# Spare products through the first routing of an attention and mixture-of-experts kernel, with two weight tiles loaded later and small steps in another order

## The chip, the cores and the metric

The kernel runs on one core of a Trainium2 chip. The metric is device time in microseconds (us): the time of one execution, as a median of several. The core's engines work side by side and wait for each other by semaphores: TensorE (PE in the profile, its weight loads PEld), VectorE (DVE), ScalarE (ACT), GpSimd (POOL) and SyncE (SP), which here issues most of the DMA transfers.

## The reference

Three stages follow one another, all in float32.

```python
def reference(**kwargs):
    ...
    attn_out = _attn_ref(**attn_kwargs)          # q, k, v: 4 x 8 heads x 768 x 64
    B, H, S, D = attn_out.shape
    x = np.ascontiguousarray(attn_out.transpose(0, 2, 1, 3)).reshape(B * S, H * D)
    x = _moe_ref(x=x, **moe_kwargs)              # 3072 tokens of 512, 8 experts, F = 1024
    return _moe2_ref(x=x, **moe2_kwargs)
```

`_attn_ref` is attention in chunks of 32 queries, each with a window of the keys around it and 8 memory keys. `_moe_ref` sends each token to one expert. The assignment is greedy over all 3072 x 8 logits, the largest first, and an expert is full with 384 tokens:

```python
    logits = x @ w_gate
    order = np.argsort(-logits.flatten())
    for idx in order:
        tok, e = (int(idx) // E, int(idx) % E)
        if assigned[tok] >= 0 or counts[e] >= cap:
            continue
        assigned[tok] = e
        counts[e] += 1
    ...
    for e in range(E):
        mask = assigned == e
        h = np.maximum(x[mask] @ w1[e], 0.0)
        out[mask] = h @ w2[e]
```

`_moe2_ref` sends each token to the two best of eight other experts, by noisy logits, and adds their weighted outputs.

## The kernel before, in words

Attention handles 24 tiles of 128 tokens, software-pipelined: for each tile a list of steps (scores, softmax, av, xtrans, logits, levac and so on) is issued in a fixed pattern, and its last tiles by the list `REST` (line 227), whose words are "step tile". `propose` and `tally` are steps that carry the first pieces of the first routing: VectorE's masks of the logits, and their counts on TensorE. Each tile of x leaves for DRAM in `xr`.

From there on `moe1` (line 1441) works with a planner, `Pipe` (line 73). It keeps a modelled time for each engine (`account`, `rdy`). The parts of the work are generators (`loads`, `lists1`, `gathers`, `splits`, `route` and others), and each yields the modelled time, or the condition, from which it wants to go on. `tick` lets those go on whose time has come by TensorE's modelled clock. The instructions of every engine are issued in the order in which the generators run, and each engine executes its own in that order. `until(cond, spare)` (line 197) is what the main loop does while TensorE has nothing to compute: with a `spare` tile it issues one spare product (a 128x128 tile of ones, `ones16`, times itself, into a PSUM tile that is overwritten later) and ticks; without one it only moves TensorE's modelled clock on by 50 ns and ticks. The main loop waits for the first expert's gathers without spares (line 1484), and for its tokens and weights with them.

The first routing is the `k == 0` pass of `route` (line 692). The experts are closed one after another, and a pass finds the next one to be full and the logit at which it is full, by a search over thresholds: VectorE compares all best logits `V` with a set of candidates (`GE`, in two halves for `k == 0`), TensorE counts them for each expert with 24 small products into `rps` (the masks are the stationary side, the one-hot `OH` the moving one), VectorE compares the counts with the capacity (`flf`), one product with `onesb` adds up over the partitions and spreads the sum, VectorE makes `d` and the next candidates `ci`. After the last round come `NQ` and its count, `est` (the expert's number, which SyncE reads with a TENSOR_LOAD and which sets the address of the first weights), `bE`, `at`, `T`, `bT`, and `shut`, which writes `L`, the logits with the closed expert masked off.

`lists1` (line 663) then makes the expert's token list: `l1pos` (two products), `lpos`, and in `slot_list` (line 613) the one-hots `sloh` and 24 products into `slps`; four small writes copy it into `idx`. `gather1` (line 1293) issues three indirect DMAs on GpSimd (`xg`), which fetch the tokens; for expert 0 GpSimd then writes `behind`, and SyncE reads it with a TENSOR_LOAD, so that later loads go out after the gathers. The gathered rows are transposed on TensorE (`tps`) and copied by ScalarE (`xT`).

`loads` (line 1017) brings each expert's weights in tiles `st0_0` to `st0_3` of 128 x 1024 (512 KB) for expert 0's first matrix, `st1` for its second. `split` turns them into a high and a low half in float16: ScalarE squares a tile and sums it (`junk`, `sq`), a product with `onesb` adds up (`tot`), VectorE makes a scale (`nt`, `i`, `s`, `i1c`), ScalarE copies the scaled tile to `w_0h` and so on, and VectorE or GpSimd writes the rest, `w_0l`. `mm1` multiplies `xT` with both halves into `m`; ScalarE and VectorE split the result into `hT`; `mm2_f32` (`m2f`) and `mm2` are the second products.

## Time and profile before

| | us |
|---|---|
| median of 3 runs | 1053.85 (1053.73 to 1054.35) |
| the profiled execution | 1061.16 |
| its span, first to last instruction | 1059.4 |
| TensorE busy in the span | 990.7 (94%) |
| VectorE busy | 643.4 (61%) |
| ScalarE busy | 460.4 (43%) |
| mean granted clock of TensorE | 0.969 of full speed |

Attention fills the first 130 us or so, the first routing goes on until expert 0's first product at 161 us, the first mixture of experts ends around 546 us and the second at the end of the span. In the timeline a row is a group of like instructions in succession, with its start, its time and their number; the bracket says how long the engine had been idle before it and what it then waited for. Rows of products after line 68 come from one helper that records every operation of the planner, so the tiles' names tell them apart. A granted clock of 1.00 is 2.4 GHz, one of 0.50 is 1.2 GHz.

### The profile page before, as it was taken

The page shows a single profiled execution, that of the slowest core. Times are in us where ns is not written, and L with a number is a line of the kernel's source. Part 1 is how long each engine was busy: PE and PEld are TensorE (multiplying, and loading weights), DVE is VectorE, ACT ScalarE, POOL GpSimd, SP SyncE. Part 2 cuts the span into 40 slices and gives each one's busy share as a digit, 9 for nine tenths or more (in the row PEclk, how much of TensorE's full clock was granted, in tenths as well). Part 3 has the DMA queues.
Part 4 walks back from the last instruction along what each step waited for, and adds up shares of the span by engine and source line. Part 5 has one row for each costly group of instructions (what it writes and reads, how often), then busy time and mean ns, then how long its engine had stood idle before and what let it go on. Part 6 is the DMA issues. An engine that isn't in the chain of part 4 may idle for free.

```text
span 1059.4 us, 21987 instructions
## 1 busy us (share of the span) xinstructions
PE 990.7 (94%) x8312; PEld 595.4 (56%) x8312; DVE 643.4 (61%) x2096; ACT 460.4 (43%) x817; POOL 294.0 (28%) x471
## 2 busy tenths in 40 slices
PE   7788659999999999999989999999999999999995
PEld 4666556767666675545554454555555555555552
DVE  5787876665765858696856745546455454554220
ACT  2575523544543537888225626044161441613110
POOL 6565423101102114011032223233223332232221
PEclk8998859999999999999999999999999999999998
DMA  8888842656669478967188729559185492563410
GB/s 243 250 256 254 292 149 103 220 161 171 207 212 221 122 189 246 245 202 175 41 222 233 195 103 282 99 126 268 63 237 129 126 266 72 169 120 101 110 60 30
DMA packets 147253, 184.61 MB, mean 174 GB/s; under 512 B 105558, under 2 KB 106070, under 8 KB 145608
## 3 DMA queue, kind: packets, MB, share of 16 engines
q1 hardware_dynamic: 129814, 131.74, 45.9%
q0 software_dynamic: 13872, 45.15, 14.7%
q10 hardware_dynamic: 3458, 6.30, 1.6%
q8 instruction: 66, 1.08, 0.4%
q14 instruction: 43, 0.35, 0.1%
HBM read 127.10 MB, written 32.44 MB: 151 GB/s over the span
## 4 chain that ended last, share of the span: by engine, by line
PE 75%; DVE 9%; DMA 7%; issue 4%; ACT 2%; SPq 2%; POOL 0%; ACTq 0%; DVEq 0%; POOLq 0%
PE m L68 58%; PE m2f L68 10%; PE rps L68 3%; DMA v<-vctx_dram 3%; DMA k<-kT_dram 2%; PE sb L304 1%; SPq L280 1%; DVE sloh L68 1%; PE slps L68 1%; DMA st<-x_dram 1%; PE xb L346 1%; ACT junk L68 1%; SPq L278 1%; DVE hT L68 1%; DMA out_dram<-pv,ts 1%
## 5 line engine op out<-in xcount | busy, mean ns | idle before, releaser
L68 PEld LDWEIGHTS <-hT 128*128 128x128 f16 (+2 forms) x1800 | 143.5, 98 | 161.0 <-issue 5.6
L68 ACT ACTIVATE hT<-m 128x384 f16<-128x384 f32 (+2 forms) x152 | 75.0, 499 | 283.2 <-PE m L68 259.4
L68 DVE SCALAR_TENSOR_TENSOR hT<-m,hT 128x384 f16<-128x384 f32 (+2 forms) x152 | 86.6, 571 | 107.2 <-ACT hT L68 92.6
L68 ACT ACTIVATE junk<-st 128x1024 f16<-128x1024 f32 x108 | 113.6, 1052 | 63.3 <-DMA st<-w_dram 35.0
L68 PE MATMUL m2f<-st,hT 128*128 128x256 f32 x480 | 127.6, 398 | 0.5 <-ACT hT L68 0.5
L68 POOL DMA_INDIRECT out_dram<-pv,ts x47 | 48.4, 1030 | 266.7 <-DVE pv L68 93.6
L68 DVE SCALAR_TENSOR_TENSOR pv<-m,ys,pv 128x512 f32<-128x512 f32 (+2 forms) x47 | 33.5, 714 | 112.0 <-PE m L68 112.0
L68 PE MATMUL m<-xT,w_3h 128*128 128x384 f16 (+2 forms) x384 | 98.3, 337 | 2.2 <-DVE hT L68 2.2
L68 PE MATMUL m<-xT,w_0h 128*128 128x384 f16 (+2 forms) x384 | 96.6, 331 | 3.2 <-DMA xT<-xg 3.2
L68 PE MATMUL m<-xT,w_2h 128*128 128x384 f16 (+2 forms) x384 | 97.3, 333 | 1.7 <-DVE hT L68 1.7
L68 PE MATMUL m<-xT,w_1h 128*128 128x384 f16 (+2 forms) x384 | 96.4, 331 | 0.0
L68 PEld LDWEIGHTS m2f<-st,hT 128*128 128x128 f32 x480 | 83.3, 190 | 10.2 <-ACT hT L68 0.9
L68 PE MATMUL m<-w_2h,hT 128*128 128x512 f16 (+2 forms) x300 | 72.2, 345 | 1.4 <-issue 1.4
L68 PE MATMUL m<-w_3h,hT 128*128 128x512 f16 (+2 forms) x300 | 71.7, 345 | 1.4 <-DVE hT L68 1.4
L68 PE MATMUL m<-w_0h,hT 128*128 128x512 f16 (+2 forms) x300 | 72.1, 346 | 0.0
L68 PE MATMUL m<-w_1h,hT 128*128 128x512 f16 (+2 forms) x300 | 71.5, 345 | 0.0
L68 PE MATMUL m<-xT,w_3l 128*128 128x384 f16 (+2 forms) x192 | 64.4, 335 | 0.0
L68 PE MATMUL m<-xT,w_2l 128*128 128x384 f16 (+2 forms) x192 | 64.0, 333 | 0.0
L68 PE MATMUL m<-xT,w_1l 128*128 128x384 f16 (+2 forms) x192 | 63.6, 331 | 0.0
L68 PE MATMUL m<-xT,w_0l 128*128 128x384 f16 (+2 forms) x192 | 63.5, 331 | 0.0
L68 POOL DMA_INDIRECT xg<-x,rows x54 | 54.2, 1004 | 29.7 <-issue 13.6
L68 POOL DMA_INDIRECT xg<-xr,idx x24 | 24.4, 1017 | 127.6 <-issue 37.6
(336 smaller groups left out, 1874.0 us busy)
## 6 DMA issues: line engine op xcount, KB each, us to landing
st<-w_dram SPq DMA_DIRECT2D x64, 512.0 KB
st<-x_dram SPq DMA_DIRECT2D x64, 512.0 KB
xr<-rb SPq DMA_DIRECT2D x24, 264.0 KB
x<-rb SPq DMA_DIRECT2D x24, 264.0 KB
v<-vctx_dram SPq DMA_DIRECT2D x12, 520.0 KB
v<-vctx_dram SPq DMA_DIRECT2D x24, 260.0 KB
q<-qT_dram SPq DMA_DIRECT2D x12, 512.0 KB
out_dram<-zero ACTq DMA_DIRECT2D x24, 256.0 KB
```

Of the source, the lines that this page charges most:

```text
L68: return f(*args, **kw)
L278: nc.sync.dma_start(behind[:, n : n + 1], flown[-AHEAD])
L280: nc.sync.dma_start(out, src)
L304: nc.tensor.matmul(sc[CH * c : CH * c + CH, hp], q[:, hp, CH * o : CH * o + CH], k[:, :, hp, k0 : k0 + KEYS], start=True, stop=True,)
L346: nc.tensor.matmul(X[hp // 2 if i == G - 1 else 0][CH * c : CH * c + CH, 0 if i == G - 1 else hp // 2, 2 * (hp % 2) : 2 * (hp % 2) + 2, :] ...
```

## The change

Ten small hunks. `until` has an option `wide`, with which a spare product has 256 columns; the main loop's wait for the first gathers now uses it, so TensorE gets spare products between the steps of the first routing. `REST` has steps `idle n`, n products of 128 x 512 each (17 in all). `slot_list` for expert 0 is issued 600 ns earlier by the model. Two of the four `idx` writes of expert 0 go to ScalarE. `est` and `bE` are written by GpSimd instead of VectorE, for all experts. The copy `dgh` moves behind the first step of `tables` (which writes `df`, now from PSUM). `T` and `bT` of the first two passes move behind `shut`. The third and fourth tile of expert 0's first weights are loaded after its gathers.

```diff
-    def until(self, cond, spare=None):
+    def until(self, cond, spare=None, wide=False):
...
             if spare is None:
                 self.t["p"] += 50.0
+            elif wide:
+                self.P.matmul(
+                    spare[:, :256].rearrange("p (a n) -> p a n", a=2), self.ones,
+                    self.ones.unsqueeze(1).to_broadcast([128, 2, 128]), start=True, stop=True,
+                )
             else:
                 self.P.matmul(spare[:, :128], self.ones, self.ones, start=True, stop=True)
...
-    "ptrans 23 av 22 logits 19 split 21 norm 22 av 23 xtrans 20 norm 23 xtrans 21 split 22 logits 20 split 23 "
-    "xtrans 22 logits 21 levac 19 propose 0 propose 0 propose 0 xtrans 23 logits 22 tally 0 logits 23 propose 0 levac 23"
+    "ptrans 23 av 22 logits 19 split 21 norm 22 av 23 xtrans 20 norm 23 xtrans 21 idle 2 split 22 logits 20 split 23 "
+    "xtrans 22 idle 2 logits 21 levac 19 propose 0 propose 0 propose 0 xtrans 23 idle 1 logits 22 idle 4 tally 0 logits 23 "
+    "propose 0 idle 8 levac 23"
...
+        def idle(n):
+            if not rest:
+                rest.append(psT.tile([128, HP, 128], F32, tag="pt", name="idle"))
+            for _ in range(n):
+                nc.tensor.matmul(
+                    rest[0], ctx.ones16, ctx.ones16.unsqueeze(1).to_broadcast([128, HP, 128]), start=True, stop=True
+                )
...
-def slot_list(ctx, pi, na, low, ids, late=0.0):
+def slot_list(ctx, pi, na, low, ids, late=0.0, soon=0.0):
...
-    yield pipe.rdy("p", oh, r) + late
+    yield pipe.rdy("p", oh, r) + late - soon
...
-        ps = yield from slot_list(ctx, pi, 4 * na, 32, ctx.tokid)
+        ps = yield from slot_list(ctx, pi, 4 * na, 32, ctx.tokid, soon=0.0 if k else 600.0)
         for q in range(4):
-            V_.tensor_scalar(
-                ctx.idx1[32 * q : 32 * q + 32, k], ps[:, :, 0].rearrange("p (a q) -> p q a", q=4)[:, q],
-                float(NTOK // 2), None, op0=ALU.add,
-            )
+            at, got = ctx.idx1[32 * q : 32 * q + 32, k], ps[:, :, 0].rearrange("p (a q) -> p q a", q=4)[:, q]
+            if k or q < 2:
+                V_.tensor_scalar(at, got, float(NTOK // 2), None, op0=ALU.add)
+            else:
+                pipe.S.activation(at, got, AF.Copy, bias=float(NTOK // 2))
...
-            V_.tensor_scalar(ctx.est[:, k : k + 1], m8[:1], -1.0, float(E), op0=ALU.mult, op1=ALU.add)
+            pipe.G.tensor_scalar(ctx.est[:, k : k + 1], m8[:1], -1.0, float(E), op0=ALU.mult, op1=ALU.add)
...
             dgh = tl([128, E], F32, "dgh")
-            V_.tensor_copy(dgh, dg)
-            dg = dgh
             tables = top(dg, plan.shifts[1], slice(off[1], off[2]), slice(off[2], off[-1] + 1))
             next(tables)
+            V_.tensor_copy(dgh, dg)
             next(tables)
...
-        V_.tensor_scalar(bE, ctx.e8f, m8, -2.0 * BIG, op0=ALU.is_equal, op1=ALU.mult)
+        pipe.G.tensor_scalar(bE, ctx.e8f, m8, -2.0 * BIG, op0=ALU.is_equal, op1=ALU.mult)
...
+        else:
+            yield lambda: k in ctx.listed or k and ctx.spread > 1
+            shut()
         V_.tensor_tensor(T, above, at, op=ALU.add)
...
-        if k < 2:
-
-            yield lambda: k in ctx.listed or k and ctx.spread > 1
-            shut()
...
         for j in range(4):
+            if i == 0 and j == 2:
+                yield lambda: 0 in ctx.gathered
...
-            pipe.until(lambda: 0 in ctx.gathered)
+            pipe.until(lambda: 0 in ctx.gathered, ps, True)
```

Where the planner's order changes is best seen in the instructions. First TensorE in one round of expert 0's search: `GE` and `rps` are the masks and their counts (24 of each pair), `flf` with `onesb` the adding product, `m1` the PSUM tile that the spares overwrite. Before:

```order
L68 LDWEIGHTS GE_0_2710
L68 MATMUL rps_0_2714<-OH0_89,GE_0_2710 31x8
L68 LDWEIGHTS onesb_66
L68 MATMUL rps_0_2741<-flf_92,onesb_66 128x8 [waits DVE_49]
L68 LDWEIGHTS GE_0_2747 [waits DVE_49]
L68 MATMUL rps_0_2751<-OH0_89,GE_0_2747 31x8
```

After:

```order
L68 LDWEIGHTS GE_0_2749
L68 MATMUL rps_0_2764<-OH0_89,GE_0_2749 31x8
L68 LDWEIGHTS ones16_64
L68 MATMUL m1_2673<-ones16_64 128x256
...
L68 LDWEIGHTS onesb_66
L68 MATMUL rps_0_2796<-flf_92,onesb_66 128x8 [waits DVE_49]
...
L68 LDWEIGHTS GE_0_2802 [waits DVE_49]
L68 MATMUL rps_0_2817<-OH0_89,GE_0_2802 31x8
```

At the first "..." stand four more spare pairs (5 in all), at the second eleven. Before the first adding product stand 15; after the search 10, 11, 12 and 23 stand before NQ's count, `rk`, `l1pos` and `slps`.

Second ScalarE after attention: `zero` is written to the output, `junk0` are the Square passes on expert 0's first weights, `w0_0h` the scaled copies, `tps` the transposed tokens. Before:

```order
L1473 DMA out_dram<-zero_2648 128x512 x2
L68 ACTIVATE junk0_0_2948,sq_0_2917<-st0_0_2905 128x1024
L68 ACTIVATE junk0_1_3027,sq_0_2917<-st0_1_2907 128x1024
L68 ACTIVATE w0_0h_3030<-st0_0_2905,s1_0_2918 128x1024
L1473 DMA out_dram<-zero_2648 128x512
L68 ACTIVATE w0_1h_3060<-st0_1_2907,s1_0_2918 128x1024
L68 ACTIVATE xT0_2979<-tps_3113 128x8x128
```

After:

```order
L1488 DMA out_dram<-zero_2666 128x512 x2
L68 ACTIVATE idx1_83<-slps_3101 32x3 x2
L68 ACTIVATE junk0_0_3132,sq_0_3027<-st0_0_3019 128x1024
L68 ACTIVATE junk0_1_3211,sq_0_3027<-st0_1_3021 128x1024
L1488 DMA out_dram<-zero_2666 128x512
L68 ACTIVATE w0_0h_3214<-st0_0_3019,s1_0_3028 128x1024
L68 ACTIVATE w0_1h_3244<-st0_1_3021,s1_0_3028 128x1024
L68 ACTIVATE xT0_3130<-tps_3260 128x8x128
```

The two idx writes now stand ahead of both Square passes, and the rest of the row is as it was.

Third ScalarE around expert 5's hidden tiles, at 410 us in the trace of before: `hT` are its copies of the products `m1`, `junk12` the Square passes on a later expert's weights, `w11` the copies of a second matrix, `rb2` scaled results of an earlier expert. Before:

```order
L68 ACTIVATE w11_3h_6972<-st11_3_6839,s2_11_6948 128x1024
L68 ACTIVATE junk12_1_7005,sq_12_6952<-st12_1_6852 128x1024
L68 ACTIVATE rb2_40_6964<-y40_6837,y3_s_6958 128x512
L68 ACTIVATE hT_7020<-m1_6985 128x384
L68 ACTIVATE hT_7041<-m1_7023 128x384
```

After:

```order
L68 ACTIVATE rb2_40_7100<-y40_7005,y3_s_7094 128x512
...
L68 ACTIVATE w11_3h_7121<-st11_3_7007,s2_11_7107 128x1024
L68 ACTIVATE hT_7144<-m1_7105 128x384
L68 ACTIVATE junk12_0_7148,sq_12_7111<-st12_0_7018 128x1024
L68 ACTIVATE hT_7208<-m1_7146 128x384
L68 ACTIVATE hT_7239<-m1_7219 128x384
```

An `hT` copy now stands directly behind the last w11 copy, ahead of the Square pass, and `rb2` stands ahead of the four w11 copies. TensorE's own order is the same in both kernels in the second half of the program.

## Rows read from the trace of the kernel before

**Rows 1.** The page's 40 slices: TensorE's busy tenths, and its granted clock in tenths.

```profile
PE   7788659999999999999989999999999999999995
...
PEclk8998859999999999999999999999999999999998
```

**Rows 2.** Windows: stretch, us, each engine's busy us (instructions), PEclk, DMA share, GB/s.

```profile
124.00:125.00 1.00, 0.64 (x12) 0.55 (x12) 0.90 (x7) 0.96 (x3) 0.00 (x0) 0.68 1.02 382
155.00:156.00 1.00, 1.00 (x20) 1.00 (x19) 0.97 (x3) 0.03 (x1) 1.00 (x3) 0.96 0.96 331
125.00:155.00 30.00, 12.55 (x212) 11.02 (x213) 22.17 (x106) 4.67 (x7) 3.79 (x7) 0.50 0.49 173
```

**Rows 3.** Timeline, one round: start us, us, engine, line, operation, out<-in, shapes, count [idle<-releaser].

```profile
134.34 1.00 DVE L68 TENSOR_TENSOR GE<-V,ci 128x372 f16<-128x372 f32 x2
...
134.94 0.87 PEld L68 LDWEIGHTS <-GE 128*31 128x31 f16 x24 [1.50 <-DVE GE L68]
...
136.15 0.16 PE L68 MATMUL rps<-flf,onesb 31*128 31x8 bf16 x1 [0.24 <-DVE flf L68]
...
136.35 0.17 DVE L68 TENSOR_REDUCE d<-rps 128x1 int32<-128x8 f32 x1 [0.25 <-PE rps L68]
...
136.78 1.00 DVE L68 TENSOR_TENSOR GE<-V,ci 128x372 f16<-128x372 f32 x2
```

**Rows 4.** Timeline, a round of expert 1's search at the full clock.

```profile
164.00 0.68 PEld L68 LDWEIGHTS <-GE 128*7 128x7 f16 x24 [0.32 <-DVE ohb L68]
...
165.06 0.33 PE L68 MATMUL m<-xT,w_0h 128*128 128x384 f16 x1
...
165.32 0.17 PE L68 MATMUL rps<-flf,onesb 7*128 7x8 bf16 x1
...
165.53 0.17 DVE L68 TENSOR_REDUCE d<-rps 128x1 int32<-128x8 f32 x1 [0.24 <-PE rps L68]
```

**Rows 5.** Pace of products: the timeline's 12 of 128 columns, the chain's 20 of 384.

```profile
160.39 0.67 PEld L68 LDWEIGHTS <-ones 128*128 128x128 f16 x12
...
269.24 3.26 PE m L68 x20
```

**Rows 6.** Timeline, start and end of expert 0's search.

```profile
130.79 0.17 DVE L68 COPY dgh<-rps 128x8 f32<-128x8 f32 x1 [0.86 <-DMA behind<-xr]
...
143.45 0.20 PE L68 MATMUL rps<-flf,onesb 31*128 31x56 bf16 x1 [0.24 <-DVE flf L68]
```

**Rows 7.** Timeline, from expert 0's list to its first product.

```profile
150.01 1.06 ACT L68 ACTIVATE junk<-st 128x1024 f16<-128x1024 f32 x1 [24.80 <-DMA st<-w_dram]
...
150.84 0.64 DVE L68 TENSOR_SCALAR idx<-slps 32x3 int32<-32x3 f32 x4 [0.57 <-PE slps L68]
...
151.78 1.18 POOL L68 DMA_INDIRECT xg<-xr,idx  x1 [18.11 <-DVE idx L68]
...
152.46 1.13 ACT L68 ACTIVATE w_0h<-st,s 128x1024 f16<-128x1024 f32 x1
...
153.82 1.42 DVE L68 SCALAR_TENSOR_TENSOR w_0l<-st,s,w_0h 128x512 f16<-128x512 f32 x2
...
156.70 0.62 PE L68 MATMUL tps<-id,xg 128*128 128x128 f16 x8
...
158.64 0.97 DVE L68 TENSOR_TENSOR GE<-V,c_consts_dram 128x360 f16<-128x360 f32 x1
...
161.07 0.49 PE L68 MATMUL m<-xT,w_0h 128*128 128x384 f16 x2
```

**Rows 8.** Timeline, TensorE's wait for expert 1's tokens.

```profile
200.43 0.62 PE L68 MATMUL tps<-id,xg 128*128 128x128 f16 x8 [1.61 <-DMA xg<-xr,idx]
```

**Rows 9.** Timeline, two stalls of TensorE, and the window around the second.

```profile
329.07 0.70 PE L68 MATMUL m2f<-st,hT 128*128 128x256 f32 x2 [0.55 <-ACT hT L68]
...
413.48 0.49 PE L68 MATMUL m<-xT,w_2h 128*128 128x384 f16 x2 [1.72 <-DVE hT L68]
...
410.00:420.00 10.00, 8.28 (x61) 4.57 (x60) 7.22 (x17) 5.90 (x13) 6.03 (x17) 0.83 1.03 282
```

More of the change, by code (lines that the diff above doesn't have):

```diff
@@ L470, in tally @@
                 counts.pop()()
-        later, counts = [], []
+        def idle(n):
[5 more added lines that the diff above has]
+                )
+        later, counts, rest = [], [], []
         load(0)
```

## The prediction

> **What bounds the kernel now.** I read first the page's slices: TensorE is busy 94% of the span, and nine tenths or more of nearly every slice after the third. There is one hole, in slices four to six, where its granted clock also falls (8, 8, 5, 9 tenths) [rows 1]. The windows of 1 us place it: the clock is full until 124.6 us (0.68 in the microsecond from 124), half until 155.0 (0.96 in the next), and in these 30 us TensorE works for 12.6 us only, while VectorE works for 22.2 [rows 2]. This is the first routing: attention has ended, no expert's tokens are known, and TensorE counts for VectorE. The timeline of one round of that search shows who waits: VectorE writes two masks (GE, 1.00 us), 24 small products count them, VectorE compares (flf), one product with `onesb` adds up, VectorE makes the next thresholds (d, ci) and masks again, 2.43 us from mask to mask [rows 3]. The chain runs through both engines; only the parts on TensorE can gain from its clock. After the first product of expert 0 (161.07 [rows 7]) TensorE is the bound, so a shift of that product moves the end one for one, unless a later wait of TensorE swallows it. The largest such waits before the second MoE stage are 1.61 us for expert 1's tokens and 1.72 us for a hidden tile [rows 8, 9]; I know of no larger one that the changed order reaches.
>
> **The change part by part.** *Clock, first bound.* At full speed the count of 24 loads takes 0.68 instead of 0.87 us; the hand-overs do not change: from the product with `onesb` to d it is 0.21 us at the full clock (165.32 to 165.53) and 0.20 at half (136.15 to 136.35) [rows 3, 4]. So if TensorE had nothing else in its queue, a round would lose 0.17 to 0.19 us, and six of them about 1.1.
>
> *Spare products.* But the queue has something else. TensorE takes its instructions in order, and `order` puts 5 spare products between count and `onesb` product and 11 between that and the next count. Their price: 20 products of 384 columns take 3.26 us in the chain, 0.163 each, and 12 of 128 columns take 0.67, 0.056 each; a product of 256 columns lies between, at 0.109 by proportion [rows 5]. After such a row of products a switch to a small tile costs about 0.1 us (the product with `onesb` comes at 165.32, and the one before it, started at 165.06, was through at 165.22 by its pace of 0.163) [rows 4]. A round thus keeps TensorE busy for 16 x 0.109 = 1.74, plus the count 0.68 to 0.80, plus 0.06 for the adding product, plus two switches of 0.1: 2.68 to 2.80 us against 2.43. TensorE becomes the bound of the round: +0.25 to +0.37, and I take +0.30; an order that left half of the 5 hidden would give +0.17. Four such periods lie between the first `onesb` product of the search and the last at 143.45 [rows 6]: +1.2, and about +0.25 for the first count, behind 15 spares.
>
> *The copy dgh.* It stands alone ahead of df at 130.79, behind a wait of 0.86 us [rows 6] for a DMA, which whatever comes first there has to make; df takes it over, and 0.20 us go. The wait also covers what the 17 `idle` products add in the attention's last 10 us: at 0.163 x 512/384 = 0.22 us each they are 3.7 us, of which TensorE has 0.3 us free in each microsecond before 124.6 and all after it [rows 2]; I take nothing, and 0.6 us if the last mask comes late. The last `onesb` product: 143.45 + 1.2 + 0.25 - 0.20 = 144.7 (+1.26; low end +0.6).
>
> *From there to the list.* The steps on VectorE are fewer: est and bE go to GpSimd, which waits idle there, and T and bT stand behind the list. Each of these is 0.1 to 0.2 us, but VectorE is not what ends last: the products l1pos and slps stand behind 12 and 23 spares. I take +0.22 at l1pos, nothing at slps (`soon` lets them be queued earlier, and at the full clock their 24 loads take 0.68 as in [rows 4] for some 0.7 now), and 0.15 back between slps and idx. So idx begins at 150.84 + 1.36 = 152.2.
>
> *idx on two engines.* Four writes take 0.64 on VectorE [rows 7]; with two on ScalarE the gather of GpSimd starts some 0.25 us sooner after idx. The price is a new wait: ScalarE takes its instructions in order, and behind its idx stand the two Square passes (junk, 1.06 each) and the copies w_0h of expert 0's first weights. Before, the first Square ran at 150.01, 0.83 us ahead of idx, and w_0h at 152.46, 1.62 behind it; now both Squares start 0.4 after idx, and w_0h comes 2.5 behind it. Who waits: VectorE's w_0l (153.82, 2.98 behind idx; now 3.65), and behind that in VectorE's queue expert 1's V, eq, OH and GE, which ended at 159.61, and then their count on TensorE and expert 0's first product. With the same steps in between GE ends 9.44 us behind idx (before 8.77). Before, 12 spares (0.67 us [rows 5]) stood between that count and the first product; now none. First product: 152.2 + 9.44 + 0.05 + 0.70 = 162.4, **+1.4 us** against 161.07 [rows 7].
>
> *Half of the weights behind the gathers.* It frees queues for the gathers, the first of which lands 4.9 us after its issue (tps at 156.70 for the gather at 151.78 [rows 7]); if half of what the queues carry there goes, up to 1.5 us of that could go. By the sum above GE, not the gather, ends last there, so I count nothing; without that cover it would be a gain of those 1.5. The two late tiles are wanted by Square passes that stand behind the three xT copies on ScalarE, so their delay costs nothing either.
>
> *Expert 1.* TensorE waits 1.61 us for its tokens at 200.43 [rows 8]. In the new order three more second-stage products (0.245 each) and a count stand ahead of that wait, while T and bT hold back idx by about 0.36: -0.7 (from -1.3 to 0).
>
> *The stall at 413.* TensorE waits 1.72 us for hT, and the clock of the 10 us around it is 0.83, so 3.4 us ran at half and cost another 1.7 [rows 9]. ScalarE's hT there now stands ahead of a Square pass, that is up to 1.06 us earlier in its queue (a pass as in [rows 7]), while the scaled copy rb2 has only changed sides with the four w11 copies; on the other hand a smaller stall of 0.55 us at 329.07 has one copy more ahead of it. I take half of the 3.3 us, -1.6 (from -3.3 to +2, if the order turns out worse), and +0.5 for the other.
>
> Sum: 1.4 - 0.7 - 1.6 + 0.5 = -0.4. The profiled execution took 1061.16 us against a median of 1053.85; a profile adds about 7 us to both kernels, so I take the difference over as it is: **1053.4**.
>
> **A rule that speaks for more.** Rows first: in the 30 us at half clock TensorE works for less than half of the time, and VectorE's 22.2 us have nothing to do with its clock [rows 2]. The Trainium skill, "TensorE: Matmul & The Clock Gate", section "Terms", puts the price of throttled time at that time x (1 - K/N), by which 30.4 us at half would be worth 15 us. By that rule the kernel would come out near 1039; by rows 3 it can be six counts x 0.19. The rows decide for me, and the rule has a small chance below.
>
> **The rivals.** *Faster.* The first routing costs only +0.6, expert 1's wait goes (-1.3), and the stall at 413 with its slow stretch vanishes (-3.3): -4.0, 1049.8. For it: the new order of ScalarE at 413 is the better one; half of that alone brings the sum to the bound. Against: the stalls are many, and VectorE's queue there is as long as before. The page's rule: every step of the routing would have to shrink by half, 15.2 us, 1038.6; against it, the hand-overs that are the same at both clocks [rows 3, 4].
>
> *Slower: the spares run at half.* If the clock falls at the end of attention, in spite of the `idle` products, the spares cost 0.22 each in place of 0.109: a round is 16 x 0.22 + 0.87 + 0.3 = 4.7 us against 2.43. Before, the clock came back 3.8 us after TensorE had been filled from 151.2 on [rows 2, 7], so this lasts for about two rounds: +3 to +4 us at the first product, and the end at 1056 to 1058 as expert 1's wait gives 0.7 back or less. It decides between 130.0 and 132.5: TensorE has little there but the wait at 130.79 and the first mask. For it: at 124.6 the clock fell although TensorE had been busy for 0.64 of the microsecond [rows 2]; against it: 15 spares stand right there. This is also how the change would fail to do what it says: there would be spares, and no full clock.
>
> **How the numbers follow.** A threshold of 0.2% (2.1 us: about what a measurement of this kernel can tell from no change) puts faster below 1051.7 and slower above 1056.0. My forecast, within that: 0.46. Faster by the two stalls: 0.30; by the page's rule: 0.02. Slower by the spares at half: 0.13, and by a stall at 413 or after it that grows (+2 and more on the first routing's +1.4): 0.09. Faster 0.32, same 0.46, slower 0.22. The range takes in the low bound of all terms, 1049.8, and +4 at the first product with 0.7 given back, 1057.0; each side leaves about 1 in 10.
>
> **What would show it.** In the changed kernel's slices the clock of slices five and six should stand at 9 or 8; a round should be 2.6 to 2.8 us from mask to mask, and TensorE, not VectorE, what flf's product waits for. The first product of expert 0 should stand near 162.4, w_0h 2.5 us behind idx. The wait for expert 1's tokens should be below 1.0, the stall near 413 below 1.0 with a clock over 0.9 in its 10 us. Wrong is the forecast if the round is shorter than 2.43 (then the spares hide), if the clock is half after 132 (then they double), or if the two stalls are where they were.

## The result and the profile after

The changed kernel took 1063.97 us as the median of 5 runs (1059.44 to 1065.94) against 1053.73 for the kernel before (1050.83 to 1054.35), a ratio of 1.0096 with a 95% interval of 1.0068 to 1.0124: some 10 us slower, outside the stated range. Two further measurements gave 1.0113 (1.0098 to 1.0128) and 1.0087 (1.0053 to 1.0122). The profiled execution of the changed kernel took 1063.97 us, with a span of 1062.1.

The page's slices of the changed kernel answer to [rows 1]; the first line is TensorE's busy tenths, the second its granted clock:

```profile
PE   6788898999999999999989999999999999999995
...
PEclk9899999999999999999999999999999999999998
```

The hole is filled and the clock is full in slices five and six, as the change says. The mean granted clock rose from 0.969 to 0.987, and the kernel became slower all the same. So the higher clock gave back less than the change cost, and the cost has to be found.

The timelines of three executions of the changed kernel and of two of the kernel before, cut at the same instructions, show where:

| stretch, us | before, two traces | changed, three traces |
|---|---|---|
| start of df, the first step of the search | 131.0, 131.8 | 136.3, 132.5, 133.2 |
| from df to the last product of the search | 12.5, 12.4 | 15.4, 14.2, 14.2 |
| from there to idx | 7.4, 7.4 | 7.4, 7.4, 7.4 |
| from idx to the first product of expert 0 | 10.2, 10.7 | 10.9, 11.3, 10.9 |
| expert 0 | 50.6, 50.7 | 49.2, 49.2, 49.2 |
| expert 3 | 47.0, 46.6 | 49.1, 50.7, 49.1 |
| expert 4 | 45.8, 45.8 | 46.9, 46.7, 46.7 |
| expert 5 | 36.9, 35.2 | 33.9, 33.9, 33.9 |
| all eight experts, 0 to 7 | 342.8, 342.1 | 342.6, 344.0, 342.4 |
| from there to the wait for the second stage's other tokens | 42.3, 41.5 | 44.4, 44.3, 44.3 |
| the last two rows together, the middle stretch | 385.1, 383.6 | 387.0, 388.3, 386.7 |

The last rows need a word. The 546 us at which the first mixture of experts was said above to end is not its end. An expert of the first stage has 384 tokens; in the first trace of before, products of 448 columns begin at 503.83, and they are the first part of the second stage's first expert (`moe2` gives that part 448 tokens). At 546.18 TensorE begins the second part, behind a wait for its tokens:

```profile
503.83 0.54 PE L68 MATMUL m<-xT,w_0h 128*128 128x448 f16 x2
...
546.18 0.48 PE L68 MATMUL m<-xT,w_0h 128*128 128x384 f16 x2 [3.24 <-DMA xT<-xg]
```

So the expectations below, where they speak of the last expert and of the way to the second stage, mean the time up to this wait.

Two things got longer: the routing, by 2 to 3 us, and the middle stretch, by 2 to 5, half and more of it in the second stage's first part. The eight experts together took 0 to 1.6 us longer than the mean of before: two of their waits went as forecast, and others came. Behind the middle stretch both kernels issue the same products, a few of them in another place.

### The profile page after: what moved, and what is told of

Same layout as the page of the kernel before. It is cut to its first block, busy times and chain, and to the rows that moved or that the text cites. A ratio compares the mean times of both kernels' runs of the same rounds, so it can differ in the third digit from the quotient of the medians.

```text
span 1062.1 us, 22418 instructions
## 1 busy us (share of the span) xinstructions
PE 1006.6 (95%) x8530; PEld 609.1 (57%) x8530; DVE 643.7 (61%) x2080; ACT 462.3 (44%) x819; POOL 298.6 (28%) x484
## 4 chain that ended last, share of the span: by engine, by line
PE 74%; DMA 10%; issue 7%; DVE 5%; SPq 2%; ACT 2%; POOL 1%; POOLq 0%; DVEq 0%; ACTq 0%
PE m L68 58%; PE m2f L68 9%; DMA v<-vctx_dram 3%; PE rps L68 3%; DMA k<-kT_dram 2%; DMA xg<-xr,idx 1%; PE sb L310 1%; PE xb L352 1%; PE slps L68 1%; SPq L286 1%; DMA q<-qT_dram 1%; DMA xr<-rb 1%; SPq L284 1%; PE pt L339 1%; DVE hT L68 1%
## 5 line engine op out<-in xcount | busy, mean ns | idle before, releaser
L68 ACT ACTIVATE junk<-st 128x1024 f16<-128x1024 f32 x108 | 113.6, 1052 | 41.7 <-DMA st<-x_dram 26.8
L68 POOL DMA_INDIRECT out_dram<-pv,ts x47 | 49.1, 1044 | 251.3 <-DVE pv L68 97.9
L68 POOL DMA_INDIRECT xg<-x,rows x54 | 53.7, 995 | 30.6 <-issue 12.2
L68 POOL DMA_INDIRECT pv<-out_dram,tg x47 | 46.0, 980 | 55.2 <-DMA out_dram<-pv,ts 31.3
```

The costliest lines, as they stand in the source:

```text
L68: return f(*args, **kw)
```

## The experiments

Ratios are to the kernel before on the same chip, with 95% intervals. The ratio of one kernel differed by up to 0.3% between two chips (0.9930 and 0.9961 for the control below), so smaller differences between runs on two chips tell nothing. "Middle stretch" is the time of the table's last row.

**What executions differ by.** The kernel before, again, and the changed kernel twice more, unchanged.

> The kernel before, unchanged, to see what one kernel's executions differ by. In the two traces at hand the attention of the changed kernel ends 5.3 us later (df at 136.31 against dgh at 130.79) although it issues the same instructions up to its last tiles, and the time of the profiled execution of before (1061.16) lies 7 us over its median. Theory A (the attention's length varies from execution to execution with its loads of keys, whatever the kernel): this trace shows an attention that is off by 2 us or more from the first trace, and the time follows it. Theory B (the attention is slower because of the change): this trace has dgh near 130.8 again, within 1 us, and a time of 1051 to 1055.

> The changed kernel, unchanged. Theory A: df anywhere from 130 to 136, and the time after attention the same as in the first trace (from df to the end 925.8 us) within 1 us; the ratio to before over 5 rounds stays near 1.01 only if the routing itself costs it. Theory B: df near 136.3 again and a ratio of 1.007 to 1.012. Theory C (the routing is what costs): from df to the first product of expert 0 about 33.6 us again, against 30.3 from dgh in before.

> The changed kernel, a third time. From df to the end 926 to 928 us in two traces; where its attention ends is what differs by execution (df at 136.3 and 132.5). If the attention is chance: df between 128 and 134 and a ratio of 1.006 to 1.009, which is what the routing (+3) and the later order (+4) explain. If the changed kernel has a longer attention: df above 133 and a ratio of 1.010 to 1.012.

The kernel before against itself: 1.0021 (1.0003 to 1.0040), so 0.2% is the least that such a comparison tells. Its profiled execution took 1054.49 us with a span of 1052.7, and every timed run lies 1.8 us over its span. A profile does not add 7 us; the first trace was simply a long execution, by 6.6 us behind the middle stretch (below). By itself this trace (dgh at 131.64) came out as theory B had it; one trace does not decide.

The end of attention moves by several us from one execution to the next. The last scores tile, in the timelines of the longest and of the shortest attention, the second from the changed kernel with half of the spares, whose instructions are the same up to there:

```profile
117.04 1.08 PE L310 MATMUL sb<-k,q 128*32 128x128 f32 x32
```

```profile
109.93 1.08 PE L311 MATMUL sb<-k,q 128*32 128x128 f32 x32
```

Up to there TensorE waited for the loads of k for 21.4 us in the first and 16.0 in the second, most of the difference. Over 18 traces the tile starts at 109.9 to 117.0. Theory A holds for single traces. The three traces of the changed kernel have it at 117.0, 114.5 and 115.0, all above the mean of 113.6. From df to the end they took 925.8, 928.0 and 925.8 us; the second has 1.6 us more at expert 3 (below).

**Spares.** The changed kernel without them, and the kernel before with them alone.

```diff
-            pipe.until(lambda: 0 in ctx.gathered, ps, True)
+            pipe.until(lambda: 0 in ctx.gathered)
```

> The changed kernel with the wait of the first routing as in before (no spare products there), all else changed. Theory C (spares cost 0.36 us a round by standing in TensorE's queue, and a round at half clock 1.6): from df to the first product of expert 0 3 us shorter than in the changed kernel, the ratio to before about 1.005 to 1.007. Rival D (a moved step costs, idx on ScalarE or the later loads): that stretch stays within 1 us of the changed kernel's and the ratio at 1.01. Theory B: the ratio stays at 1.01 and df at 136.

> The kernel before with the wide spare products in the first routing and nothing else. Theory C: a round of the search 2.7 to 2.8 us against 2.43, the first product of expert 0 3 to 4 us later than in before, the ratio to before 1.003 to 1.004. If the full clock were worth more than the spares cost: a round below 2.43 and a ratio below 1. Rival D: within 0.2% of before.

Without the spares: 1.0059 (1.0047 to 1.0072), round 2.42 us, from df to the first product 30.6. With the spares alone: 1.0051 (1.0030 to 1.0073), round 2.79, 34.7. The spares cost about 0.5%, by the routing, as theory C had it; but without them a loss of 0.6% is still there, which is not in the routing.

A round of the changed kernel's search in the second trace, at the full clock, answers to [rows 3]:

```profile
139.71 0.80 PE L68 MATMUL rps<-OH,GE 128*31 128x8 f16 x24
...
140.44 0.72 PE L68 MATMUL m<-ones 128*128 128x256 f16 x5
140.55 0.15 DVE L68 TENSOR_TENSOR flf<-rps,capB 31x8 bf16<-31x8 f32 x1 [0.47 <-PE rps L68]
...
141.09 0.17 PE L68 MATMUL rps<-flf,onesb 31*128 31x8 bf16 x1
...
141.20 1.38 PE L68 MATMUL m<-ones 128*128 128x256 f16 x11
...
142.51 0.80 PE L68 MATMUL rps<-OH,GE 128*31 128x8 f16 x24
```

From count to count it is 2.80 us (139.71 to 142.51). The comparison flf waits for the count at 140.55, and the adding product could follow at once, but stands behind the 5 spares until 141.09; the next count stands behind 11. TensorE is the bound, as the sum said.

In two of the four traces of kernels with all spares and the `idle` products the clock still fell, for a round or two. Windows of 2 us of the first trace of the changed kernel (columns as in [rows 2]):

```profile
138.00:140.00 2.00, 2.00 (x32) 1.49 (x29) 1.19 (x7) 0.00 (x0) 0.65 (x3) 0.86 0.03 8
140.00:142.00 2.00, 2.00 (x15) 1.20 (x13) 1.37 (x4) 0.00 (x0) 0.00 (x0) 0.50 0.51 191
142.00:144.00 2.00, 2.00 (x35) 1.61 (x34) 0.52 (x4) 0.00 (x0) 0.00 (x0) 0.79 0.20 73
144.00:146.00 2.00, 2.00 (x37) 1.60 (x35) 1.28 (x4) 0.00 (x0) 0.00 (x0) 1.00 0.03 8
```

From adding product to adding product that round took 4.07 us.

To have the price of the spares with all later instructions equal, a control was needed, since the planner answers every edit with another order. Writing two idx on ScalarE, alone, happens to give exactly the later order of the kernel with spares alone.

```diff
-            V_.tensor_scalar(
-                ctx.idx1[32 * q : 32 * q + 32, k], ps[:, :, 0].rearrange("p (a q) -> p q a", q=4)[:, q],
-                float(NTOK // 2), None, op0=ALU.add,
-            )
+            at, got = ctx.idx1[32 * q : 32 * q + 32, k], ps[:, :, 0].rearrange("p (a q) -> p q a", q=4)[:, q]
+            if k or q < 2:
+                V_.tensor_scalar(at, got, float(NTOK // 2), None, op0=ALU.add)
+            else:
+                pipe.S.activation(at, got, AF.Copy, bias=float(NTOK // 2))
```

> The kernel before with two of the four idx writes on ScalarE and nothing else. By the planner this gives, after the first routing, instruction for instruction the order of the run with spares alone on TensorE, ScalarE and VectorE, but no spares: so it is that run without its spares. Theory G (the spares cost by themselves, and that later order is 3 us shorter than before's): from df to the first product of expert 0 about 30.6 to 31.2 us against 34.7 with spares, from there to the second stage 380 to 381 us, and the ratio 0.996 to 0.999. If the later order were worth nothing: ratio 1.000 to 1.002.

> Two idx writes on ScalarE alone, again. It was 0.993 of before on a chip on which before took 1061.6; by its trace the stretch from the first product of expert 0 to the second stage was 382.3, against 383.6 to 385.1 in before, which explains 1 to 3 us of 6.5. If the gain holds: 0.993 to 0.997. If it was that chip: 0.998 to 1.001.

> Spares alone on the kernel before, again, beside its control without spares (b_idx2: the same later order) on the same chip. If the spares cost what the traces show in the routing (df to the first product 34.7 against 29.7): 4 to 6 us, 0.4 to 0.6%, between the two. If they also cost elsewhere: 8 us or more between the two medians, and the trace must show a stretch outside the routing that is longer.

On one chip the control took 1051.62 us (0.9961, 0.9938 to 0.9984) and the spares alone 1059.15 (1.0034, 1.0012 to 1.0056): 7.5 us for the spares. (The pair differs in the idx writes too; behind idx the traces differ by 0.6 us.) In the traces of this pair the middle stretch is 381.3 in both, and from df to the first product it is 30.2 against 35.2: 5 us of the 7.5. Without the `idle` products the clock is at half when the search begins (0.50 from 130 to 138 in this trace), so the price is higher than in the changed kernel. The control is also faster than before, on both chips (the other 0.9930, 0.9905 to 0.9955), though on that chip before itself took 1061.6.

**Half the spares.** Each spare counts 110 ns more in the planner's model:

```diff
+                self.t["p"] += 110.0
```

> The changed kernel with about half the spares in the first routing (80 of 256 columns instead of 146: 3 between count and adding product, 6 between that and the next count), all later orders the same. If the spares cost by filling TensorE's queue: a round is 2.3 to 2.4 us instead of 2.79, the last product of the search comes 12.2 to 12.5 us behind df instead of 14.2, and the ratio is 0.002 lower than the changed kernel's, near 1.009. If they cost in another way (a later order, contention): the ratio stays at 1.011.

> The kernel before with half of the wide spares in the first routing (83 instead of 155) and nothing else; all later orders are those of the run with spares alone, which had a ratio of 1.005. If the spares cost by filling the queue: round 2.3 to 2.4 us instead of 2.79, first product of expert 0 about 2 to 3 us earlier than with all spares (31.5 to 32.5 us behind df instead of 34.7), ratio 1.001 to 1.003. If the loss is the later order or the attention: ratio 1.004 to 1.006 again.

The expected 2.3 to 2.4 us came in neither. The changed kernel with half of them: 1.0063 (1.0038 to 1.0088), a first round of 2.54 while the clock was still full, then 2.89 to 3.01. The kernel before with half: 1.0035 (1.0014 to 1.0056), 2.88 and then 3.00. These rounds with 9 spares are longer than one with 16 at the full clock, because the clock is at half in them. Windows of 2 us, first the kernel before with half of the spares, then with all:

```profile
132.00:134.00 2.00, 2.00 (x31) 1.37 (x29) 1.74 (x6) 0.00 (x0) 0.67 (x3) 0.50 0.14 51
138.00:140.00 2.00, 2.00 (x31) 1.38 (x30) 1.33 (x5) 0.00 (x0) 0.00 (x0) 0.50 0.00 0
146.00:148.00 2.00, 2.00 (x15) 1.11 (x14) 1.28 (x11) 0.00 (x0) 0.00 (x0) 0.50 0.00 0
150.00:152.00 2.00, 2.00 (x18) 1.65 (x17) 1.79 (x11) 0.00 (x0) 0.00 (x0) 0.79 0.71 233
```

```profile
130.00:132.00 2.00, 2.00 (x11) 1.45 (x10) 1.28 (x6) 0.00 (x0) 0.52 (x1) 0.50 0.95 358
132.00:134.00 2.00, 2.00 (x33) 1.40 (x32) 1.44 (x5) 0.00 (x0) 0.65 (x3) 0.65 0.05 12
138.00:140.00 2.00, 2.00 (x36) 1.47 (x35) 0.95 (x4) 0.00 (x0) 0.00 (x0) 1.00 0.00 0
146.00:148.00 2.00, 2.00 (x25) 1.80 (x23) 1.97 (x17) 0.00 (x0) 0.00 (x0) 1.00 0.00 0
```

With half of the spares TensorE is busy in the records for 2.00 of 2 us from 132 on, and the clock is 0.50 until about 150.

**The idle products.** Without them and without spares, and alone on the kernel before.

```diff
-    "ptrans 23 av 22 logits 19 split 21 norm 22 av 23 xtrans 20 norm 23 xtrans 21 idle 2 split 22 logits 20 split 23 "
-    "xtrans 22 idle 2 logits 21 levac 19 propose 0 propose 0 propose 0 xtrans 23 idle 1 logits 22 idle 4 tally 0 logits 23 "
-    "propose 0 idle 8 levac 23"
+    "ptrans 23 av 22 logits 19 split 21 norm 22 av 23 xtrans 20 norm 23 xtrans 21 split 22 logits 20 split 23 "
+    "xtrans 22 logits 21 levac 19 propose 0 propose 0 propose 0 xtrans 23 logits 22 tally 0 logits 23 propose 0 levac 23"
```

> The changed kernel with the first wait as in before (no spares) and the REST list of before (no idle products); the small steps and the later loads stay, and TensorE's and ScalarE's order after the first routing is that of the changed kernel. Without spares alone the ratio was 1.0059. Theory E (what is left of the loss is the planner's order after the first routing: the stall of 2.05 us for hT at expert 3 and a wait of 6.3 us ahead of the second stage, 59 spares and 3.0 idle, where before had 4.6): ratio again 1.004 to 1.007, expert 3 at 49.1 us and the last expert at 44 us. Theory F (the idle products of the attention's tail cost about 3 us): ratio 1.002 to 1.003, and the last scores tile starts near 111 to 113 us instead of 115.

> The kernel before with the 17 idle products in the attention's tail and nothing else; every later order is that of before. In the traces so far the last scores tile starts at 114.5 to 117.0 us in three of four kernels with these products and at 111.0 to 113.4 in those without, though no instruction differs up to there. If the idle products cost: last scores tile at 114 or later and a ratio of 1.002 to 1.003. If that difference is chance: 111 to 114, ratio within 0.002 of 1; the stretch from the last scores tile to flh 17.3 us instead of 17.6 to 18.1.

1.0056 (1.0035 to 1.0076) without both, as with the idle products (1.0059); alone on before 0.9987 (0.9958 to 1.0015), with the last scores tile at 112.4 and 17.3 us from there to flh, against 17.6 to 18.1 in before. They cost nothing that these runs show.

**The later order.** With est and bE back on VectorE from the third pass on, with and without spares; and est and bE on GpSimd alone on the kernel before.

```diff
-            pipe.G.tensor_scalar(ctx.est[:, k : k + 1], m8[:1], -1.0, float(E), op0=ALU.mult, op1=ALU.add)
+            (V_ if k > 1 else pipe.G).tensor_scalar(ctx.est[:, k : k + 1], m8[:1], -1.0, float(E), op0=ALU.mult, op1=ALU.add)
...
-        pipe.G.tensor_scalar(bE, ctx.e8f, m8, -2.0 * BIG, op0=ALU.is_equal, op1=ALU.mult)
+        (V_ if k > 1 else pipe.G).tensor_scalar(bE, ctx.e8f, m8, -2.0 * BIG, op0=ALU.is_equal, op1=ALU.mult)
```

> The changed kernel without spares, with est and bE of the third pass and later written by VectorE as in before. The order of TensorE after expert 3 then differs: 10 spares after the first product of expert 0 instead of 69. Theory E: the stall at expert 3 and the longer wait ahead of the second stage go, expert 3 takes about 46.6 and the last expert 41 to 42 us; ratio 1.000 to 1.003. Theory F: the ratio stays at 1.006.

> The changed kernel in full, spares too, with est and bE on VectorE from the third pass on: the later order is that of the run n_est2. If the two causes add (spares about 4 to 5 us, the later order about 7): ratio 0.006 to 0.008 lower than the changed kernel's 1.011, so 1.003 to 1.006; first product of expert 0 32.5 to 33.7 us behind df, from there to the second stage 380 us instead of 387 to 388. If est and bE on GpSimd are not the cause: 1.010 again.

> The kernel before with est and bE on GpSimd in all passes and nothing else. It has a later order of its own, with no spares at all after the first product of expert 0. If est and bE on GpSimd cost by themselves (VectorE waits for them, a later load): each expert of the first stage is 0.3 us or more longer, ratio above 1.003. If what costs in the changed kernel is the one order that the planner reaches there: no stall of 2 us at expert 3, first product to second stage 379 to 384, ratio 0.995 to 1.002.

Without spares the ratio falls from 1.0059, or 1.0056 on the same chip, to 0.9991 (0.9972 to 1.0009), and the middle stretch from 386.5 to 380.1: 6.4 us, more than expected. With spares, 1.0023 (0.9994 to 1.0051) and a middle stretch of 380.3, against 387 to 388 in the changed kernel. But est and bE on GpSimd in all passes, alone on before, are at 0.9991 (0.9966 to 1.0016) with a middle stretch of 383.4. So GpSimd doing them costs nothing by itself that these runs show; what costs is the order that the planner reaches when they are combined with the other edits.

Of the 6.4 us, 5.8 lie in the second stage's first part (43.9 to 38.1) and 0.6 in the eight experts. (In this trace the part behind it took 37.3 us instead of 33.7; no run tells why, and the timed runs decide.) What is wrong with that order shows in two places. First ScalarE around expert 3, in the second trace of the changed kernel:

```profile
327.97 0.72 ACT L68 ACTIVATE rb<-y,y_s 128x512 f16<-128x512 f32 x1
...
329.29 1.15 ACT L68 ACTIVATE w_0h<-st,s 128x1024 f16<-128x1024 f32 x1 [0.59 <-DVE i1c L68]
...
330.35 1.13 ACT L68 ACTIVATE w_1h<-st,s 128x1024 f16<-128x1024 f32 x1
...
331.39 1.13 ACT L68 ACTIVATE w_2h<-st,s 128x1024 f16<-128x1024 f32 x1
...
332.43 1.13 ACT L68 ACTIVATE w_3h<-st,s 128x1024 f16<-128x1024 f32 x1
...
333.47 0.56 ACT L68 ACTIVATE hT<-m,i1c 128x384 f32<-128x384 f32 x1
...
334.08 3.53 PE L68 MATMUL m2f<-st,hT 128*128 128x256 f32 x10 [2.04 <-ACT hT L68]
```

The same place in the second trace of before:

```profile
324.19 1.14 ACT L68 ACTIVATE w_0h<-st,s 128x1024 f16<-128x1024 f32 x1
...
325.64 0.58 ACT L68 ACTIVATE hT<-m,i1c 128x384 f32<-128x384 f32 x1 [0.31 <-PE m L68]
...
326.12 1.14 ACT L68 ACTIVATE w_1h<-st,s 128x1024 f16<-128x1024 f32 x1
...
329.34 0.57 ACT L68 ACTIVATE hT<-m,i1c 128x384 f32<-128x384 f32 x1
...
329.97 0.70 PE L68 MATMUL m2f<-st,hT 128*128 128x256 f32 x2 [0.55 <-ACT hT L68]
```

In the changed kernel ScalarE writes the scaled copy rb, waits 0.59 us for a scale, and writes four weight copies, 1.05 us apart, in one block before the hidden tile hT that TensorE wants: 2.04 us of stall. In before one hT stands between w_0h and w_1h, so that three copies are in the block, and the stall is 0.55. Behind the longer stall the clock fell for 3.4 us in the second trace, and expert 3 took 50.7 us; in the other two it did not fall, and expert 3 took 49.1. Like stalls for hT came at expert 4 (0.94) and expert 7 (1.27), where before has none.

Second GpSimd's queue, ahead of the second stage's second part. Its tokens come by three gathers (`xg`), and a finished tile of the first part is written out by an indirect DMA too (`out_dram<-z`). The changed kernel, first trace:

```profile
542.24 1.00 POOL L68 DMA_INDIRECT xg<-x,rows  x1 [2.33 <-DVE lmkey L68]
545.33 1.02 POOL L68 DMA_INDIRECT out_dram<-z,ts  x1 [2.10 <-DVE z L68]
546.65 0.99 POOL L68 DMA_INDIRECT xg<-x,rows  x1 [0.30 <-issue]
547.95 0.96 POOL L68 DMA_INDIRECT xg<-x,rows  x1 [0.30 <-issue]
...
550.50 3.47 PE L68 MATMUL m<-ones 128*128 128x128 f16 x59
556.95 0.48 PE L68 MATMUL m<-xT,w_0h 128*128 128x384 f16 x2 [2.98 <-DMA xT<-xg]
```

The run with est back on VectorE and no spares in the routing:

```profile
533.50 0.98 POOL L68 DMA_INDIRECT xg<-x,rows  x1 [0.43 <-DVE lmkey L68]
534.79 0.94 POOL L68 DMA_INDIRECT xg<-x,rows  x1 [0.30 <-issue]
536.03 0.94 POOL L68 DMA_INDIRECT xg<-x,rows  x1 [0.30 <-issue]
...
544.00 0.48 PE L68 MATMUL m<-xT,w_0h 128*128 128x384 f16 x2 [0.22 <-DMA xT<-xg]
```

In the changed order the write stands ahead of two gathers and waits 2.10 us for VectorE's z, so the last gather starts 35.4 us behind the first part's first product; in the run with est back it is 30.1. In before the write stands between the second and the third gather, which starts at 32.8 to 33.2. In all of these traces the second part's first product follows the last gather by 8.0 to 9.1 us. Ahead of it TensorE of the changed kernel has 59 spares by the plan and then waits another 2.98, where before had 21 and waited 2.4 to 3.2; in the run with est back it has no spares there and waits 0.22.

**idx on VectorE alone.**

```diff
-            if k or q < 2:
+            if True:
```

> The changed kernel without spares, with est and bE on VectorE from the third pass on, and with all four idx writes of expert 0 on VectorE; later order as in the run n_est2 (ratio 0.9991). From idx to the first product of expert 0 that run took 11.0 us, before 10.2 and 10.7. If the two writes on ScalarE hold back the Square passes and w_0h: 10.3 to 10.6 here, w_0h 1.6 to 2.1 us behind idx instead of 3.1, and the ratio 0.0005 lower, 0.997 to 1.000. If the later loads are what holds them back: 11.0 and 3.1 again.

0.9936 (0.9916 to 0.9956), on the chip where before took 1061.6 and the control had 0.9930, so the ratio does not tell. w_0h came 2.0 us behind idx instead of 3.1, and GE ended 9.0 behind it instead of 10.2, but the first product came 11.0 behind idx, as with two writes on ScalarE. So the new wait on ScalarE is real and is not what ends last there. What does is the gathers: TensorE waited for the second one's tokens,

```profile
159.59 0.62 PE L68 MATMUL tps<-id,xg 128*128 128x128 f16 x8 [0.95 <-DMA xg<-xr,idx]
```

and from there to the first product at 162.60 had no gap, with 23 spares, the last transposes and the count of expert 1's masks in its queue.

## Why the prediction was wrong

*The views were read rightly but for a trifle, and the price of a round was right.* (0.68 in the microsecond from 124 puts the fall of the clock at 124.4, not 124.6; no term uses it.) 2.68 to 2.80 us were forecast for a round with spares, 2.79 was measured; TensorE became the bound of the search. By the mean clocks, (1 - 0.969) x 2 x 1059 = 66 us at half became 28. The rule of the Trainium skill ("TensorE: Matmul & The Clock Gate", section "Terms"), throttled time x (1 - K/N), would make that worth 19 us, as an estimate; this case does not bear it out, for with the spares and the new order the kernel took 10 us more.

*The term for the routing was too small.* From df to the first product the sum had +1.6 us; the three traces have +3.4, +2.5 and +2.1 on the mean of before. The search itself takes 14.2 us where it would have been 13.9 by the sum, and 15.4 with one round at half clock, the slow rival's mechanism in small (4.07 us, as against its 4.7). From idx on, rows of the first trace of the changed kernel, which answer to [rows 7]:

```profile
159.12 0.31 DVE L68 TENSOR_SCALAR idx<-slps 32x3 int32<-32x3 f32 x2 [0.51 <-PE slps L68]
...
159.84 0.16 ACT L68 ACTIVATE idx<-slps 32x3 int32<-32x3 f32 x1 [0.15 <-issue]
...
162.26 1.13 ACT L68 ACTIVATE w_0h<-st,s 128x1024 f16<-128x1024 f32 x1
```

```profile
167.64 0.61 PE L68 MATMUL tps<-id,xg 128*128 128x128 f16 x8
167.92 0.98 DVE L68 TENSOR_TENSOR GE<-V,c_consts_dram 128x360 f16<-128x360 f32 x1
168.09 1.22 PE L68 MATMUL m<-ones 128*128 128x128 f16 x19
169.24 0.79 PE L68 MATMUL rps<-OH,GE 128*15 128x8 f16 x24
169.97 0.50 PE L68 MATMUL m<-xT,w_0h 128*128 128x384 f16 x2
```

w_0h starts 3.1 us behind idx, not 2.5, and the first product 10.9 behind it; over the three traces that is 0.4 to 0.8 more than the mean of before, where 0.0 was forecast. GE ended 9.3 to 9.8 us behind idx, near the forecast's 9.44, but it was not what ended last: the count behind it stands in TensorE's queue behind 19 spares, which follow the last gather's transposes. It started 0.3 us behind the end of GE in this trace, 1.2 and 0.8 in the others. The prediction had GE and not the gathers end last, and saw the 12 spares behind the count go, but not the 19 ahead of it.

By the timed pair, the spares cost even 5.7 us in the changed kernel (1.0113 against 1.0059 on one chip, each within 1.5 us or so); with est back on VectorE it is 3.4 (1.0023 against 0.9991, on two chips). Of this the traces place 2 to 3 in the routing and 0.5 ahead of the second part.

*Expert 1 and the stall at 413 came as forecast or better.* The wait for expert 1's tokens is gone (expert 0's stretch 50.6 to 49.2: -1.4 against -0.7). The stall at 413, a row of the first trace of the changed kernel, which answers to the second of [rows 9]:

```profile
421.98 0.48 PE L68 MATMUL m<-xT,w_2h 128*128 128x384 f16 x2 [0.40 <-DVE hT L68]
```

1.72 fell to 0.40, and the clock does not fall there; expert 5's stretch went from 36.9 or 35.2 to 33.9, against a forecast of -1.6. (35.2 is the second trace of before, in which the clock did not fall behind the same stall: the other 1.7 us that the prediction counted there are not in every execution.)

*The step that failed is the later order.* The sum had +0.5 for the stall at 329 [rows 9] and nothing for what lay behind. Measured, against the mean of before: +2 to +4 at expert 3, +0.9 at expert 4, +1.3 at expert 7, which took back what experts 0 and 5 gave, and +2.4 in the second stage's first part, where the sum had nothing. The middle stretch is 2 to 5 us longer where the sum had 1.8 us less. The one copy more ahead of hT at 329 had been seen, and was sized too small: the stall grew by 1.5 us, and the clock fell behind it in one trace of three. The other waits are new. I had compared the orders where before had a wait, and not where the new order could make one: a block of four weight copies ahead of a tile that TensorE wants can be read from ScalarE's order, and a write that waits for VectorE ahead of two gathers from GpSimd's. The rival with a stall that grows (0.09) came nearest, but it named 413, the stall that shrank.

*Together.* By the timed runs the two causes account for the change: spares 1.0113 to 1.0059, the order after them 1.0059 to 0.9991 (on another chip). By the traces 2 to 3 us of the spares' price have no place; the intervals leave room for that. Attention ended later in all three traces of the changed kernel, but it also ends late in single traces of others: the nine traces of kernels made from the changed one have the last scores tile at 114.2 in the mean, the nine made from before at 112.9, and single ones of the former spread by 7. Whether that is chance is left open.

*The 7 us that a profile was to add* were no such thing, but one long execution; no term of the sum hung on it.

## What to carry to other kernels

Filling an engine's idle time with products to hold its clock is a purchase: where the engine takes its instructions in order, each product stands ahead of the next real one, and a faster clock gives back only what the engine itself does on the chain. Here a count fell from 0.96 to 0.80 us, and the round still grew from 2.43 to 2.79. Where a planner sets the order, a small edit early on must be costed by the whole order that it leads to, engine by engine: look for blocks of long instructions, or one that waits itself, ahead of a short one that another engine waits for. And an effect of an edit is best measured against a control with the same later order.

## What the runs showed of the hardware

TensorE can be busy in the records without a break and stay at half clock: from 132 to 150 us with 9 spares of 256 columns and 25 small products a round, at 0.50, while with 16 spares a round it was 1.00 from 134 on in the same place. And the same instructions of the attention took from 109.9 to 117.0 us up to the last scores tile in 18 executions, with 16.0 us of TensorE's waits for the loads of k in the shortest and 21.4 in the longest, so that a single trace tells nothing of a few us there.
